# A written order of 3,500 steps, and a table of which half tile is masked where, exchanged for another of the same pieces

## The chip, the cores and the metric

The kernel runs on one core of a Trainium2 chip. The time is device microseconds of that core for one execution. Before the change it is 446.86 us, the median of 3 runs (444.54 to 447.4). The engines are TensorE (PE in the profile, with its weight loads as PEld), VectorE (DVE), ScalarE (ACT), GpSimd (POOL) and SyncE (SP), whose queue issues nearly all DMAs.

## The reference

Attention with a threshold, and then a maxout feed-forward layer, all in float32 at the interface:

```python
# q, k, v: 8 batches x 8 heads x 576 rows x 64
scores = (1 / sqrt(64)) * q @ k.T
thresh = max(scores, axis=-1, keepdims=True) - tau          # tau = 0.02
scores = where(scores >= thresh, scores, -1e9)
attn = exp(scores - max(scores)); attn = attn / (sum(attn) + 1e-9)
x = (attn @ v) with the heads side by side                  # 4608 tokens x 512
h = maximum(maximum(x @ w1, x @ w2), x @ w3)                # 768 wide
out = h @ w_out
```

## The kernel before

**Tiles and stages.** Two by two, 16 groups of four heads (a quad; two quads are one batch) go through attention. A step is 128 query rows of a pair of heads, and has two half tiles of 128 x 576 scores, one for each r; there are 144 steps and 288 half tiles. PE transposes q and k (tile `tp`, evacuated to `qt` and `kt`; `qs` is `qt` with its partition halves exchanged), and makes the scores (`sc`) of a half tile in one of four PSUM banks. DVE copies them, negated, to SBUF (`z`) and takes the row's extreme in the same instruction. ACT makes the exponentials. POOL multiplies by the reciprocal of the sum into `P` (bf16), a DMA transposes `P` into `ptq` (nine DMAs for one quad), and PE multiplies with v (`o`, evacuated to `xt`). From four such products a batch's x is complete, and the feed-forward layer runs in 18 pieces of hidden width (`ph`, three for each 128 of the width, evacuated to `hm`, `hm` and `hT`), then as products with w_out (`po`, to `ob`, stored to `out`). The last batch is done in two parts, so that it has 36 smaller pieces.

**How a half tile is masked** is one digit for each of the 288 in the table `MASKED`:

| digit | DVE | ACT | POOL | reads the bank after DVE's pass |
|---|---|---|---|---|
| 0 | maximum, threshold | two passes (Prelu, Exp) | | nobody |
| 2 | maximum | two passes | | ACT's first pass |
| 1 | maximum, mask-and-sum | one pass | | nobody |
| 3 | maximum, mask-and-sum | one pass | | ACT's pass |
| 5 | maximum, threshold, mask-and-sum | one pass | | ACT's pass and DVE's second |
| 4 | maximum, threshold | one pass | two instructions (`far<-z,th`, `z<-z,far`) | nobody |

In the code these are `masked` (L368), `on_pool` (L371), `direct` (L374), `threshold` (L400), `exponents` (L416), `marked` and `moved` (L434, L440) and `numerators` (L462). The mask-and-sum of DVE is one `scalar_tensor_tensor` that reads `z` twice (digits 1 and 3) or the bank and `z` (digit 5). In the first two quads (`loose`, L364) no reciprocal is taken: the exponentials go straight to `P`, and the sums come from products with `ones`.

**The order.** A string, `ORDER`, is walked from left to right; each letter issues the next piece of its kind. All engines' instructions are tied to their engine's order (`_Ordered`), so the string sets what stands behind what on PE, DVE, ACT, POOL and in SP's queue. The letters that matter here: `S` a half tile's scores with the bank's number, `T` transposes, `O` a product with v, `F` and `B` the two halves of a piece of the feed-forward layer; `m` maximum, `s` threshold, `k` mask-and-sum, `e` and `n` the passes of ACT, `G` ACT's pass of a half tile that POOL has masked; `b` and `C` POOL's two masking instructions, `p` POOL's normalizing, `z` a weight cast on POOL; `t` the transposing DMA, `l` a piece of loading q, k or v, `g` a weight load, `o` a store.

```python
elif what == "m":
    c, r = line["m"].pop(0)
    maximum(c, r)
...
elif what == "t":
    turned(next(ts))
...
elif what in "pqylQ":
    next(flows[what])
```

A letter that waits holds up everything behind it on its engine or queue, and nothing on the others.

Of the kernel before, what the change touches and what calls it, by code (L numbers as in the profile page):

```python
# [48 lines left out]
ORDER = """
lllllllllT1laclT0qqalS3qqclmS2lS1mS3lsmeT0lbmT2nlS1CsalsS3amleqmlqecylGcS0snS3tymyeS2qnsmqeS0bmeS1mCeT3smlaS  # L50
2lknS1qlS0GsmS3ntqmnmbT1emtT0eCcS3anssS0mbT2eS1mqeS3mT0CGctnssmaqGktS1besS0smS3ntyS2memeyCtsnsS3mnS1myS2lGbT
0elmS3qetscT1CnmS0atmeS2qS1ssnsmbGklS0eCgmetmeqmeS1lsnsS0skbS2lemlGqmS1tnysnsS0memS2CeskT1teczO3GmnyskS1Lbsm
eS3tmCES2emT1tO0embakCeS1swnktS0nqS2GmO3ntkbGsmyT1LtCrmS0esS3cpGtS2smpeS1rsmepgmngbemlS2qnslkO3pElmCelrsS2sw
elS0mpnlO3kGpkeT2zrsS1ramLS2mpgeO3stpmnperO1sEqknqswS0LyS3meT1EztO0cesrmpeS1twpnT3mpS0aF2gsemqS3nsBzsmT1eF0r
psgchS3teyBpmS2nS1pnmF3petmBqF2nrsvBepstvS1hpS0nmS2ztnrS1smznF3mteBprsF2evpS0temF3pnBmyS1npvBgemF0lhT2rkBpng
S3valS1emF2qlesBmlpS0evT3F1snrmS2peBscpS0emF3znssmBegkO2htknO0srservpeztF1wxS3nqF2mS0eprBstnpmBnF3zvS0hgS1pe
lmF2eplrBmepgBvF0nysS1veBpmnS2F3khnzBmS1ssrevpgS0S2mtpnT3kepF1mBanmT3qS0tevzT2ssrS1mazteS2mS0ncpS1tesrF3mqek
pteS2smnBprmntprmeS1yS0septmF2upssmuqelT3kS1yelS0smnBlprnslpmlnO1kqleprcO0tupuepS2twnS3ymS1xmepF0sS2nrsmpBnm
yS3hbS1smeF2ptT0meF3ysaBskT1elqrF0rvnBlCcBelS2vhlF1pGmS0tpBersmqT3eS2vtpS0ameF1pssF3mnbBknBpF2rhvT0tBnpcS3ey
svF1tnS0mCBersS2tvnF3pmnS1ptBremF0yhsmpS2GtS3spsmF1epBmnoBqsrveS2lqF3eslvS0petmBpnS1mF2phrmS0eptS3smnS1pBmey  # L60
S0snmF3bemF1tCBnsvBnkF0teF2rsrvpBhBepvS1etbO3mnpvnO1psrkeptS2xwS0GpmT1S3arCtsmS2nmF1eqokGplS3eS0rslmeBplmnpl
srmS2uptS3umS0qnT1moF2ebskleCtT3ersBmecpaS0kupT1uO3mepctO2GkqnrsrleS1wplS0xmS3qlnF2mpteBsmpeS0kT1phS3nsmN2ap
mtnrkpS0jsS3rtrsemF2yeS1mBonyssmpS3eF0vptS1nsmyBepF2rmnptS3vnS1psmeBtqsS0meF3pshsrS1mlpnBmlS2epS0svlepF1lmnT
3bBtmnF2qvnF0BrcepS1hsrT3splBmepF2lassvS1CnlS3metS0pBmnF1vnqS3remqT2BespcF0hslBmpGS2lvbS3elrmS1pntF0mCeF2mT3
eBskptBavS1eF3ssqhmT0nBysS1nvtF2yncyT3BqerrF0vpaBGpmS2tS3hpmF1ntqF0rsmeBpnBvptO3esvpeO2rklpnlerS1pwxtS0nymS3
emS2tyyeS1mqS0nmF3pemplesmF1leklnsBrktpekeS0pS2umuBetmnrT3kpO2uorssknlpO0erlcupriS3wxS1pemF2tpnS0myeBmS1ohyS
3slpemT2S0lepmF1tnpsmF3aBrkpBnsvS0teF2rbsmnS1BpvnS0shCmS3temS2epS1smtnF0pmT3GyBmbF2nrsrvS1eptBssmeCF0ceT1lBa
pvlF3hF1kptGBsBnrvpF2nrS0vpteS3mpS1eBmptnF0smqhS3sreBpmS1nptvF2eS3mqT0nBsmqleF1vqlS3ecBpleS2srmtnpS0mhpO3snm
tO2ekekT1ywxF0arS2rssyS3nbmF1eBmynplBvnS2plsF3svepT0tmBnpS1chCS2tresmF0S3empF1GmBqnT2srsvBpaS3rveptS0meqS1mS
2npS3meF0ptmepsnssmT2tS1qncBbekleCO2lsmunlrrO3skulqerlS0pwxlS1GpmoS3F2emptnspsmS1nprBnmpesrpS3uF1pumS0tnpBme  # L70
F2bF3hsBpeoS0veCS1tmnBN2myetssrekyS1vjpF0tGmS2pnBrkptS3hF1smeS0yminpBrsF3svebT2tBmaCS1vnS2snmbS0emS3pF1GsmS2
pemBCtnF0mF3hsrrssT2pnBcpT1eBvlpaS2evF0pF1GmqT3BnlcBhrlkS2peF3lvS0eprtmBnS1mqnF2tsrqsS0meBqveF1tpmhS3npBssmF
0eptvT2S3parkF1etqBemBS2qvhS3nsmpS1S0empF2nrsstmF3peBmbeS1skBnCsO0mervnO1pGvptrS2wxpS3nmytS1ersmS0ynyF2mplem
plnS1spetS0mT3epBrscnptmepT3S1katO0uqrsumqeO3lkpnoeS1wyS2xmS0npT3mF1elcetrsmS3pnBkeplmelS0ysursF2kptuS3meBpm
S0hF1syrkepT3oS2matBpessS3mF0nqvF2nqrsmBtnBpsvnF1pS3rhBbemF0tevS2pS3epmF1nCBtmeF2srsvBnbS3knS0phmBGF1pmeF3sC
rtsBrveBnvT2pS0hcS1pGF3mptF2emBpnsS0rsvptnS1mpT3eBrmaF0tpeS3vpS1nsmBtqnF2ssmqhT3BrebscS0eS1vpF3nmpF2nBsmCteB
rvS1hS0psnmF2pGmBtT1ervT3pS0acF2pnS1mtqT3smT0aqBecS3qS1veqS0nmF2emerskS3peBmepmnS1ktbF0ussrkuepoS3remBpmeCS1
nsS2umO3pukGpoO1ersmpeS2twpnS0smyxO3tnrsmyO2epskntynS1rwpS0ermN3tbxmnCssS1jF2pGmiS3peBsrmS0pthS1sepmF3nF2pts
mBnpF0sveS1treS3pmeBpsF1metbBnsvF3ChBnBvO2nbrvS1nCwS0GmF3S2rpGmS1psmBeF0pstrshmBpeS2sveS1tbmS3nCF0mnF2snsS1m
pBGsmpBeF3rrstbvF1hBnCF0veBpGBvS2phrS3npmtO1epsmF0xptF2nsBebrF1vBnCBvS3hpS0GmF1ptF2rmepBnsBptvO0epvO3ntwS1xr  # L80
S0pmF3psmtbF2seCkBGBurpupoF1uF0thF3uvF1vF0hoF2vF1vF3hF2vF0vF1hF3vF0vF2hF3vF0vF2hF1vN0vO3jO2iwO1xO3wF2xF1uF3h
oF2vF1vF0hF3vF1vF2hF0vF3vF2hF1vF3vF2hF1vF0vF3hF2vF1vN3uoF2jiF1uofd
"""


# [895 lines left out]
```

## Time and profile before

| | |
|---|---|
| median of 3 runs | 446.86 us |
| profiled execution, time | 447.12 us |
| profiled execution, span | 445.3 us |
| granted TensorE clock | 1.00 in every stage |
| PE, weight loads | 424.0 us (95%), 312.6 us (70%) |
| DVE | 385.6 us (87%) |
| ACT | 400.6 us (90%) |
| POOL | 360.7 us (81%) |
| DMA packets | 88.50 MB, mean 199 GB/s |

Busy time is that of one profiled execution. In a table of stages the share of busy time tells which engine sets a stage's length; in a list of instructions in order of time, the square bracket is the idle time of the engine before the instruction and what ended it. Source lines are of no use here, since every instruction of these engines is recorded at the helper's line L102: the groups are told apart by their tiles.

### The profile page before, as it was taken

The page shows a single profiled execution, that of the slowest core. Times are in us where ns is not written, and L with a number is a line of the kernel's source. Part 1 is how long each engine was busy: PE and PEld are TensorE (multiplying, and loading weights), DVE is VectorE, ACT ScalarE, POOL GpSimd, SP SyncE. Part 2 cuts the span into 40 slices and gives each one's busy share as a digit, 9 for nine tenths or more (in the row PEclk, how much of TensorE's full clock was granted, in tenths as well). Part 3 has the DMA queues.
Part 4 walks back from the last instruction along what each step waited for, and adds up shares of the span by engine and source line. Part 5 has one row for each costly group of instructions (what it writes and reads, how often), then busy time and mean ns, then how long its engine had stood idle before and what let it go on. Part 6 is the DMA issues. An engine that isn't in the chain of part 4 may idle for free.

```text
span 445.3 us, 14407 instructions
## 1 busy us (share of the span) xinstructions
PE 424.0 (95%) x5268; PEld 312.6 (70%) x5270; DVE 385.6 (87%) x1217; ACT 400.6 (90%) x824; POOL 360.7 (81%) x460
## 2 busy tenths in 40 slices
PE   7777899999999999999999998999999999999996
PEld 6454457766678776877688676787688876786873
DVE  4999999989899999998999895899899998887442
ACT  3999999999999999999999897999999999996431
POOL 2898999778999898899797897899989889898100
PEclk9999999999999999999999999999999999999999
DMA  7999999999999999999999999999999867659412
GB/s 176 266 212 244 215 300 237 222 222 290 209 223 161 243 228 249 221 241 222 203 238 235 173 217 251 249 197 182 157 247 184 136 107 177 132 97 139 129 38 83
DMA packets 213959, 88.50 MB, mean 199 GB/s; under 512 B 189184, under 2 KB 202240, under 8 KB 213888
## 3 DMA queue, kind: packets, MB, share of 16 engines
q1 hardware_dynamic: 213360, 86.96, 96.3%
q8 instruction: 41, 0.67, 0.6%
q10 hardware_dynamic: 528, 0.62, 0.5%
q14 instruction: 30, 0.25, 0.2%
HBM read 35.65 MB, written 9.44 MB: 101 GB/s over the span
## 4 chain that ended last, share of the span: by engine, by line
PE 69%; DVE 8%; POOL 6%; DMA 6%; issue 5%; ACT 4%; SPq 1%; POOLq 0%; DVEq 0%; ACTq 0%
PE ph L102 28%; PE sc L102 23%; PE po L102 8%; PE o L102 8%; DVE z L102 5%; POOL P L102 4%; DMA ptq<-P 3%; DMA qm<-in_q_dram 3%; PE tp L102 3%; ACT z L102 2%; POOL qs L102 1%; PE warm L102 1%; SPq L102 1%; ACT P L102 1%; POOL vb L102 1%
## 5 line engine op out<-in xcount | busy, mean ns | idle before, releaser
L102 DVE TENSOR_SCALAR_CACHE_REDUCE z<-sc 128x576 f32<-128x576 f32 x250 | 183.2, 752 | 13.7 <-PE sc L102 11.7
L102 POOL TENSOR_SCALAR P<-z,rs 128x576 bf16<-128x576 f32 x214 | 166.4, 790 | 25.1 <-DVE rs L102 12.4
L102 PE MATMUL sc<-kt,qs 64*128 64x256 f32 (+2 forms) x640 | 176.8, 412 | 5.9 <-DVE z L102 2.9
L102 PE MATMUL sc<-kt,qt 64*128 64x320 f32 (+2 forms) x640 | 178.3, 423 | 3.8 <-DVE kt L102 1.5
L102 PE MATMUL ph<-xt,w 64*128 64x288 bf16 (+2 forms) x2160 | 170.9, 283 | 0.8
L102 PEld LDWEIGHTS <-w 64*128 64x128 bf16 (+1 forms) x2160 | 125.9, 94 | 34.1 <-PE ph L102 4.4
L102 ACT ACTIVATE z<-z,th 128x576 f32<-128x576 f32 x153 | 114.7, 768 | 1.4 <-DVE th L102 1.0
L102 PEld LDWEIGHTS sc<-kt,qs 64*128 64x128 f32 (+1 forms) x640 | 91.0, 175 | 22.8 <-DVE z L102 6.3
L102 PEld LDWEIGHTS sc<-kt,qt 64*128 64x128 f32 (+1 forms) x640 | 90.5, 175 | 17.3 <-DVE z L102 6.1
L102 ACT ACTIVATE z<-z 128x576 f32<-128x576 f32 x139 | 93.6, 675 | 0.2
L102 ACT ACTIVATE z<-z,nm 128x576 f32<-128x576 f32 x73 | 55.2, 769 | 1.3 <-POOL z L102 1.2
L102 POOL COPY qs<-qt 64x640 f32<-64x640 f32 (+3 forms) x66 | 44.9, 680 | 11.4 <-ACT qt L102 8.1
L102 PE MATMUL po<-wo,hT 64*128 64x512 bf16 (+3 forms) x454 | 53.4, 354 | 0.3
L102 DVE TENSOR_TENSOR hm<-ph,hm 128x576 bf16<-128x576 f32 (+2 forms) x54 | 37.1, 687 | 14.6 <-PE ph L102 14.3
L102 POOL TENSOR_TENSOR z<-z,far 128x576 f32<-128x576 f32 x35 | 47.1, 1344 | 1.8
L102 ACT ACTIVATE hm<-ph 128x576 bf16<-128x576 f32 (+2 forms) x54 | 31.8, 590 | 11.8 <-PE ph L102 11.4
L102 PEld LDWEIGHTS <-hT 64*128 64x128 bf16 (+2 forms) x456 | 28.7, 95 | 17.8 <-issue 1.2
L102 DVE TENSOR_TENSOR hT<-ph,hm 128x576 bf16<-128x576 f32 (+2 forms) x54 | 37.1, 687 | 2.7 <-PE ph L102 0.7
L102 DVE SCALAR_TENSOR_TENSOR z<-z 128x576 f32<-128x576 f32 x46 | 38.9, 851 | 0.0
L102 PE MATMUL o<-ptq,vb 128*64 128x512 bf16 (+2 forms) x544 | 36.5, 282 | 2.1 <-DMA ptq<-P 2.1
L102 POOL TENSOR_SCALAR far<-z,th 128x576 int8<-128x576 f32 x35 | 28.6, 816 | 6.8 <-DVE th L102 4.0
L102 POOL TENSOR_SCALAR P<-stage,rs 128x576 bf16<-128x576 f32 x38 | 30.4, 807 | 3.8 <-DVE rs L102 1.6
(63 smaller groups left out, 505.8 us busy)
## 6 DMA issues: line engine op xcount, KB each, us to landing
vm<-in_v_dram SPq DMA_DIRECT2D x32, 256.0 KB, 4.9
qm<-in_q_dram SPq DMA_DIRECT2D x15, 512.0 KB, 5.3
km<-in_k_dram SPq DMA_DIRECT2D x15, 512.0 KB, 5.8
out_dram<-ob SPq DMA_DIRECT2D x14, 512.0 KB, 4.2
stage<-in_moe_w_dram SPq DMA_DIRECT2D x9, 512.0 KB, 5.1
ptq<-P SPq DMA_TRANSPOSE x144, 4.3
vr<-in_v_dram SPq DMA_DIRECT2D x16, 128.0 KB, 4.5
stage<-in_moe_w_out_dram SPq DMA_DIRECT2D x3, 512.0 KB, 4.9
```

The costliest lines, as they stand in the source:

```text
L102: ins = fn(*a, **kw)
```

## The change

The two tables are exchanged; nothing else in the program differs. The pieces of work are the same: 288 half tiles, 64 transposes, 40 products, 162 pieces of hidden width, 144 transposing DMAs, the same loads and stores. The digits of `MASKED` go, in number, from 183 to 178 (0), 53 to 58 (1), 6 to 12 (2), 3 to 5 (3), 38 to 33 (4) and 5 to 2 (5). In the first batch (the first 36 digits) they go from 16, 3, 4, 2, 10, 1 to 10, 5, 10, 3, 8, 0. The string has 3,504 signs in place of 3,522, from its tenth on in another order.

```diff
 MASKED = """
-420024032402140400004110405430000044114100451050050000000000011100000000
-110001000101000001040001004000000001141040010411001030000000000040000104
-001001001110010021004004100000010100400001001040000014100040400100000100
-014000011010010100000401400000004000101141001000400000004404004000402045
+423020132420040121044310022420204214114100451000101000010000000040100020
+012000000010110014000000040000000000441000010141001000010040100000000100
+101000001111100014001000010001004004000010011001005401004000001004000100
+114000001110000001000410400000401000101100010010404000004044010040300003
 """
...
 ORDER = """
-lllllllllT1laclT0qqalS3qqclmS2lS1mS3lsmeT0lbmT2nlS1CsalsS3amleqmlqecylGcS0snS3tymyeS2qnsmqeS0bmeS1mCeT3smlaS
...
+lllllllllT3laclT0qqalS1qqclmS3lS0mS2lS1melsmeT3lbnlsS2mCaS0lmelmeS2qlqcGT0skS1atqecqmeyS3mnS0meyyemS2lnsS3kb
...
 """
```

What this moves on the engines is shown at three places. The first is ACT at the start, from the second evacuation of k on (`tp` is the transposed q or k, `qt` and `kt` what they are evacuated to, `sc` a bank of scores, `nm` the extreme, `th` the threshold, `P` the exponentials of the first quad). Before:

```order
L102 ACTIVATE z_221<-sc_214,nm_212 128x576
L102 ACTIVATE P_260<-z_221 128x576
L102 ACTIVATE qt_183<-tp_236 128x320
L102 ACTIVATE qt_183<-tp_251 128x256
L102 ACTIVATE z_232<-z_232,th_267 128x576
L102 ACTIVATE z_249<-z_249,th_267 128x576
L102 ACTIVATE P_260<-z_211,nm_212 128x576
L102 ACTIVATE P_303<-z_232 128x576
L102 ACTIVATE z_276<-sc_263,nm_277 128x576
```

After:

```order
L102 ACTIVATE z_221<-sc_214,nm_212 128x576
L102 ACTIVATE z_233<-sc_218,nm_234 128x576
L102 ACTIVATE P_256<-z_221 128x576
L102 ACTIVATE qt_183<-tp_243 128x320
L102 ACTIVATE z_240<-z_240,th_259 128x576
L102 ACTIVATE z_264<-sc_230,nm_265 128x576
L102 ACTIVATE P_256<-z_211,nm_212 128x576
L102 ACTIVATE qt_183<-tp_294 128x256
```

Of the passes shown, three of six now read a bank of scores (`sc`) where two of seven did, and the second evacuation of q stands four instructions behind the first.

The second is SP's queue around the load of q for quad 8 (`qm_3175` before, `qm_2789` after). `ptq_2708` before and `ptq_2694` after are the transposed `P` of quad 5, `ptq_3200` that of quad 6; `ob` is a block of output. Before:

```order
L102 DMA_TRANSPOSE ptq_2708<-P_3071 128x9x128
L102 DMA out_0_dram<-ob_2295 64x2x1024
L102 DMA vm_2804<-in_v_dram 64x4x256 x2
L102 DMA q8_3176<-in_q_dram 128x4x64
L102 DMA k8_3178<-in_k_dram 128x4x64
L102 DMA_TRANSPOSE ptq_3200<-P_3143 128x9x128
L102 DMA out_0_dram<-ob_3197 64x2x1024
L102 DMA qm_3175<-in_q_dram 128x2x512
```

After:

```order
L102 DMA_TRANSPOSE ptq_2694<-P_2824 128x9x128
L102 DMA k8_2792<-in_k_dram 128x4x64
L102 DMA qm_2789<-in_q_dram 128x2x512
L102 DMA_TRANSPOSE ptq_2694<-P_2860 128x9x128
L102 DMA_TRANSPOSE ptq_2694<-P_2926 128x9x128
L102 DMA_TRANSPOSE ptq_2694<-P_3048 128x9x128
L102 DMA_TRANSPOSE ptq_2694<-P_3088 128x9x128
L102 DMA out_0_dram<-ob_2253 64x2x1024
```

The load stood behind all nine transposing DMAs of quad 5, one of quad 6 and two stores; now it stands behind five of quad 5 and ahead of the other four and of both stores.

The third is SP's queue at the end of quad 9 (`ptq_4857` before, `ptq_4827` after; `vr` is a part of v). Before:

```order
L102 DMA_TRANSPOSE ptq_4857<-P_5061 128x9x128
L102 DMA vr_5197<-in_v_dram 64x8x64 x2
L102 DMA_TRANSPOSE ptq_4857<-P_5195 128x9x128
L102 DMA_TRANSPOSE ptq_4857<-P_5230 128x9x128
L102 DMA_TRANSPOSE ptq_4857<-P_5294 128x9x128
```

After:

```order
L102 DMA_TRANSPOSE ptq_4827<-P_5109 128x9x128
L102 DMA_TRANSPOSE ptq_4827<-P_5177 128x9x128
L102 DMA_TRANSPOSE ptq_4827<-P_5209 128x9x128
L102 DMA_TRANSPOSE ptq_4827<-P_5270 128x9x128
L102 DMA vr_5343<-in_v_dram 64x8x64 x2
```

The two loads of v that stood ahead of the last three transposing DMAs of the quad stand behind the last.

More of the change, by code (lines that the diff above doesn't have):

```diff
@@ L49 @@
 ORDER = """
-lllllllllT1laclT0qqalS3qqclmS2lS1mS3lsmeT0lbmT2nlS1CsalsS3amleqmlqecylGcS0snS3tymyeS2qnsmqeS0bmeS1mCeT3smlaS
[L51 to L79, printed above, removed]
@@ L80 @@
-pBGsmpBeF3rrstbvF1hBnCF0veBpGBvS2phrS3npmtO1epsmF0xptF2nsBebrF1vBnCBvS3hpS0GmF1ptF2rmepBnsBptvO0epvO3ntwS1xr
-S0pmF3psmtbF2seCkBGBurpupoF1uF0thF3uvF1vF0hoF2vF1vF3hF2vF0vF1hF3vF0vF2hF3vF0vF2hF1vN0vO3jO2iwO1xO3wF2xF1uF3h
-oF2vF1vF0hF3vF1vF2hF0vF3vF2hF1vF3vF2hF1vF0vF3hF2vF1vN3uoF2jiF1uofd
+lllllllllT3laclT0qqalS1qqclmS3lS0mS2lS1melsmeT3lbnlsS2mCaS0lmelmeS2qlqcGT0skS1atqecqmeyS3mnS0meyyemS2lnsS3kb
+lT1emlnS0mCtaS2smT3nS1sqemT0tGsycS2akT3nqS0nmesymS1tqemqecT0tbamS3eCS0smtnmeS3T1kGS2snS0smtbemCemgnS3klnS2bl
@@ new lines @@
+mGS0tecCT3asmS1eykS3qGtsmeqmeteskS2bnS1mS0tnmqeCT2smnS3temqemS0lyGscS1lnS3mzlS2esmtebmnS0mCnlS3smnS2tnS1mbeO
+0sCmGkeS3bemtLkCS1nS2mGO0mEekT1GsrtssO3mpawpetS1kbLS0remO3tCemnsT0kgS1pEscT2gnplmaS0qeT2rlwqO1elscqGlkS3yleS
+2mplLrsS0mntpS1mnpS3reszmO2empeO0pmEgnkqS3tnwS1pLrsS2smpeT0myO3eysmEtpskaS2S1ezwetremT3pF0ecpBnsF2myzF3hsgBn
+tBqvnF0rnS2vptBermpS1hkpS2eS3mngpsrS1mnpT0mazsmS3esF0sseqrgmT1S2ntpcS3nspmF1eBysrmpBetS2vzeS3smeF0pgBnptmF2h
+zvBnF3stnrbS0vF1eCmBnBsegrF2vzlhS0GBpgF1nlmqO3etvpeO0srkqnpBwxpS2evS0ztnF3rmnpBmS1epsS0rlhmzF2elmBpnlsvF0npg
@@ new lines @@
+BleprS3vS1gepmS0tnpS2mepmS1nF3yssmF0emBeS2khT1zsnsBrmS3evtF2armBeqsT1nvT3tzS0escS2pamtS1npsS0mnF3ptmepmeT1S2
+ncS0tersS1rmpeBmqtnsmqnS0F2plureplmS1uylskBnplmelkS0qelsO1upmluprtseO3kyepS2wxS0pnmF3tnbS1rsmeBprmS2eS0CshmF
+1eT3myBatF2vnT0pT3cGBtyF1qsavS0epkF3tnS2pBnmlBhyssrsS0mlpeS1rtsnpvF2empF3eBsbmBtnrvT1qF0hcS2qeF3stqemS1npBmB
+lnpsS2vlepF1rstvS0npBmeCS3monF2slhsBmpGlS0vyF3nlrmBpelS1sveptS2rsF0mnypS3nmS1perBmyS2hspsmF3nS0ptmeBsrsmF2bn
+F1sevtpBnBpvS3etrCF0hmS2eBslmbF1elvT3CnBtsaO0vpnkO2GptrGS1pwxS3pemT2tS0nmqS1emytS3nssF0rrmpeomyeS1ylcpT3nBlm
@@ new lines @@
+palnkqS1lursS3remlF2petsmpuS1snbkT3S0eptBercpemO3CnmuO1sktpGurS0wxqoS2meS3qtmeS1psmnF0pT2emBptS3asrskF1hqS2m
+nBpmeS0S3pvntS2snprmN1eposmelpmS0elsrF3spmjlF2ekBbinS1svpS0etrmpBemS3pnS1ssmCF0hnmBF3evT1tGF2rcpBnkBpnS1rvS0
+hprmS3etT2pssF1semyBemtS0avqS3nF2smlpnS1mlBqestrF0mnqS3svnT1pBeprF2chBspmtnS1yvF3pemS2tpnT0S1meBtrsamF2evT0q
+BtecF1phS3kqT0elS2malBpnF3lvF0eqlsrBmeqtS1svnS2psBmnpF3khF1ynBtsrmBpevO2eprskeptO3vnpnlS1weyS0trmxS2pnmS3yeF
+1rympemptS2nS0pnmT3BelmelcF2elklukS0utkS3eBsrrempempO1uskptusO3erkpnoS0lrxwpS2nlmS1peF3ompS0elmBpnlsS2mhS1bt
@@ new lines @@
+ssmeS0yF3meS2meCBtmF1nF0rGssvpBBkpS2thsvF3eS0ymnBtrmpT2eS1rvpaS0mnytF2qmS3eqBssnsmS0pnvF1peT3mT2BlakS0htqF2s
+rcnF1qmeBpS3evpBemF2teF0rvpS3nskS1peBmBhrtsmS3pnF2svpeS1mF0tebBsrmnpS3veT1CBlmnO2lsnsscblO3nkphrGS0wptF1xmpT
+2eBrrCstaS0vF3nmS2peBsmpeS1F0vGptS2mepBmT3ythS1rcS2nyF0spnmF3nsprBsmeT1ytBvqeS2vpS0almnpS3lS1meqlF2rempnsmT3
+qeBklpetcS0erkS3qntmO1purusmpO0nspkeopS3xlwS2elS0rmpeF1lsmpnlsmnS2tskeF0bBerstmeykBuS2ChS3umF0nyF1osmpnBtrS2
+psGvN3permtpekS0pjBstemF3pnvS2S0nribmT1BaspmS2thS1sysreCmF0eF3mBpessBvetqS2veS1qnmS0pF3GmS2pmeBtF1mhT0rnsS2c
@@ new lines @@
+pS3epmT0BasstsF2nvbF0nmT1CBlersBclnS3pvlF1hrpmS2leBpstmnS0qF3veS2pmnBmnqF1F0vGtBknS3S2sshrmpBeF1rpveT3BpmtaS
+0evpS3emF2tqF1nmS0nrskBpS3smhBepmF2nS0ktbBerrssvpO3empeO1kptnveS0CswxS2nmS3pnmS0ytGmS1T2resrF3rpmecyynS0plmS
+2eplBsmntpmeT1qkuO0tapusO2srkepleorS1wxS3qtemS0pS2nmpF1emtqnskT3peBssrcnpmS0uS3plumF2nplF1meBtrssBphS3pnvS2l
+eyF0rmoT1eBmtpaS3svF2peS1smeqtF0mnBqkBhbS1esvS2nF3myyF0nCmS1terrS2mepBssGsF1bvBnmBphF3kpteT2F0vnBpceBCvtS1hF
+2srnrmS3pGT0BmpaF1srspevS3tS0epmF2nptBmS3npvS0emtqBnT1mqF3hsBcnbS0srsveS2CS1meS3mepF0rGsF2mpBesmptBnvF1pT3hs
@@ new lines @@
+rkBtpaS0veT2S3pmeF1ctqT0BamqS2eS0vqnS3mS1nrmF2pnsmpeT0rsmBnptkeqS3cuF1sepmutkS3esrS2epmS0onpBmnkeS2srmpuO3rs
+umpeO0opsknbeO1trweyO2xktnynS3wpN0ermptxspnS3CeF1trmS2jBspGmiS3yF0hspmS2epBtsnmS1pnF3rvS2tbesmBeCF0mnS1svS2p
+GmO3pnrssmF1petBrwpBshS2petvF3nS0pmBetmbS2nF1vCS0nssmBGF3mbS2rhsrCF0emS1eBspmF2npvBGBstbvS3eF1ChmS0nBsmpF2eF
+3spvGBntbrS0vS1epmO2mCeBxsS1khS2pnF0rrmeF3ptBmGpBssknF2ptF1evBeprBrvhF0ptnS3vpS2nmBptrO1svpeO3mptF0xwepnktF3
+rpBptBuuoF1uF0hF2uvF1voF0hF3vF2vF0hF3vF1vF0hF3vF2vF1hF3vF0vF2hF1vN0vO1jO3iwO0xO2wF3xF2uF0hoF1vF2vF3hF0vF2vF3
@@ L83 @@
+hF0vF1vF3hF0vF1vF2hF0vF3vF2hF1vF3vN1uoF0jiF1uofd
 """
```

## The prediction

> **What bounds the kernel now.** I read the page's busy line first, then the busy time by stage, then the waits of the stages in which PE is idle, and last the instructions in order of time at those waits.
>
> ```profile
> span 445.3 us, 14407 instructions
> PE 424.0 (95%) x5268; PEld 312.6 (70%) x5270; DVE 385.6 (87%) x1217; ACT 400.6 (90%) x824; POOL 360.7 (81%) x460
> ```
>
> Four engines are above 80%, so the average says little. By stage (length, then PE, PEld, DVE, ACT, POOL):
>
> ```profile
> 0.00:12.00 12.00, 9.40 (x98) 7.72 (x98) 5.96 (x26) 4.92 (x9) 4.03 (x11) 1.00 0.79 177
> 12.00:62.00 50.00, 40.47 (x406) 24.55 (x408) 48.47 (x157) 49.49 (x85) 45.76 (x54) 1.00 1.12 241
> 62.00:100.00 38.00, 37.67 (x500) 26.94 (x500) 33.88 (x107) 37.50 (x79) 31.86 (x43) 1.00 1.14 240
> 100.00:270.00 170.00, 165.52 (x2132) 122.31 (x2128) 158.76 (x505) 164.08 (x344) 151.49 (x195) 1.00 1.11 223
> 270.00:410.00 140.00, 139.75 (x1842) 109.21 (x1840) 124.86 (x396) 132.81 (x285) 124.37 (x158) 1.00 0.90 173
> 410.00:445.30 35.30, 31.17 (x306) 21.88 (x304) 13.72 (x31) 11.76 (x26) 3.18 (x4) 1.00 0.30 88
> ```
>
> From 12 to 62 us there is no feed-forward work to give PE: it idles 9.53 us, while ACT is idle 0.51 and DVE 1.53 of 50. That stretch is as long as the passes of ACT and DVE that the order puts ahead of the first feed-forward piece. From 62 us on PE is the bound. It idles 0.33 us to 100, 4.48 to 270, 0.25 to 410, and 4.13 at the end, where the change moves little. So there are two things to win: the length of the early part, and the 4.48 us. The waits of 12 to 62 us say the same of the banks, PE waiting for DVE and hardly for ACT:
>
> ```profile
> PEld sc L102 <- DVE z L102: 10.2, 15, 2.0
> PEld tp L102 <- ACT z L102: 0.7, 1, 0.7
> PE tp L102 <- ACT z L102: 0.2, 1, 0.2
> PE sc L102 <- ACT z L102: 0.2, 1, 0.2
> ```
>
> Of the 4.48 us four stalls make 4.02; each row has PE's idle time before it in brackets:
>
> ```profile
> 126.25 0.46 PE L102 MATMUL tp<-identf,qm 64*128 64x64 f32 x8 [0.73 <-DMA qm<-in_q_dram]
> ...
> 174.33 0.46 PE L102 MATMUL tp<-identf,qm 64*128 64x64 f32 x8 [0.72 <-DMA qm<-in_q_dram]
> ...
> 248.20 0.53 PE L102 MATMUL sc<-kt,qs 64*128 64x320 f32 x1 [0.51 <-POOL qs L102]
> ...
> 269.44 0.93 PE L102 MATMUL o<-ptq,vb 128*64 128x512 bf16 x11 [2.06 <-DMA ptq<-P]
> ```
>
> **The change: sums of work.** The prices are these rows (busy total, mean ns):
>
> ```profile
> L102 DVE TENSOR_SCALAR_CACHE_REDUCE z<-sc 128x576 f32<-128x576 f32 x250 | 183.2, 752 | 13.7 <-PE sc L102 11.7
> L102 ACT ACTIVATE z<-z,th 128x576 f32<-128x576 f32 x153 | 114.7, 768 | 1.4 <-DVE th L102 1.0 <-DVE rs L102 0.2
> L102 POOL TENSOR_TENSOR z<-z,far 128x576 f32<-128x576 f32 x35 | 47.1, 1344 | 1.8
> L102 DVE SCALAR_TENSOR_TENSOR z<-z 128x576 f32<-128x576 f32 x46 | 38.9, 851 | 0.0
> L102 DVE TENSOR_SCALAR th<-nm 128x1 f32<-128x1 f32 x226 | 30.4, 145 | 0.8
> L102 POOL TENSOR_SCALAR far<-z,th 128x576 int8<-128x576 f32 x35 | 28.6, 816 | 6.8 <-DVE th L102 4.0
> L102 ACT ACTIVATE z<-sc,nm 128x576 f32<-128x576 f32 x14 | 10.1, 734 | 3.7 <-DVE z L102 3.7
> ```
>
> By the digits, POOL masks 5 half tiles fewer: 5 x (0.816 + 1.344) = 10.8 us less. DVE's mask-and-sum goes from 61 to 65 (digits 1, 3, 5), 4 x 0.851 = 3.4 us more, and its thresholds from 226 to 213 (digits 0, 4, 5), 13 x 0.145 = 1.9 us less: 1.5 us more. ACT makes two passes for 190 half tiles in place of 189, one of 0.768 us more. PE's work does not change. So nothing is taken off the engine that bounds after 62 us, and the two that bound before it get a little more; what can be won is in the order.
>
> One row speaks against taking masks from POOL to DVE. A mask-and-sum on DVE and, beside it, POOL's first masking step:
>
> ```profile
> 43.34 0.75 DVE L102 SCALAR_TENSOR_TENSOR P<-z 128x576 bf16<-128x576 f32 x1
> ...
> 43.59 1.11 POOL L102 TENSOR_SCALAR far<-z,th 128x576 int8<-128x576 f32 x1 [0.51 <-DVE th L102]
> ```
>
> POOL's 0.816 became 1.11 us, 0.29 more. The digits 1 and 3, whose mask-and-sum reads SBUF twice, go from 56 to 63; at 0.29 each, 7 give POOL 2.0 us back, and its gain is 8.8 rather than 10.8. I take 8.8: it is idle time there either way, since POOL bounds neither stage. [...]
>
> **The early part.** Counted in the string up to its first `F`, before has 56 half tiles' scores and 79 large passes of ACT (`e`, `n`, `G`: 41 + 26 + 12), after 58 and 81 (45 + 26 + 10). ACT, the fullest, gets 2 x 0.768 = 1.5 us more before PE is fed, which was here:
>
> ```profile
> 69.89 0.72 PE L102 MATMUL ph<-xt,w 64*128 64x288 bf16 x8
> ```
>
> In exchange PE has two half tiles behind it, which take 0.97 us by the chain of waits:
>
> ```profile
> 347.07 0.98 PE ph L102 x16
> ...
> 350.81 0.97 PE sc L102 x8
> ...
> 368.41 2.47 PE o L102 x40
> ```
>
> Net +0.6 us. DVE's count (2 maxima, 2 masks, 9 thresholds fewer) is 1.5 + 1.7 - 1.3 = 1.9, less 0.97: +0.9, of which its idle 1.53 can take some. Ends: +0.9 at the top, and below nothing ACT's idle 0.51 in that stretch, -0.5. I take +0.6. Not in it is that direct half tiles (digits 2, 3, 5), whose bank is freed only after ACT or DVE has read it again, go from 7 to 13 in the first batch; in before PE waited 1.1 us for ACT at such places (the three ACT rows of the waits), 0.16 for each of 7, so six more are 0.9 us of PE's wait in a stretch in which PE is idle 9.5 us anyway. I take nothing; the third rival is where that fails.
>
> **The four stalls.** At 174 us the load of q for quad 8 came late, held in SP's queue behind transposing DMAs and a store:
>
> ```profile
> 165.44 2.33 SPq L102 DMA_TRANSPOSE ptq<-P  x1
> 167.87 0.62 SPq L102 DMA_DIRECT2D out_dram<-ob  x1
> 168.54 0.58 SPq L102 DMA_DIRECT2D qm<-in_q_dram  x1
> ```
>
> Between that load and the transposes that need it, the string has 5 `S`, 2 `O`, 3 `F`/`B` and 2 `T` before, 14, 4, 6 and 4 after. At 0.485 for an `S`, 1.23 for an `O` and 0.49 for an `F` or `B` (the rows above) that is 6.4 us against 14.7 without the `T`s: 8.3 us more for a load that was 0.72 late. This stall goes: -0.72.
>
> At 269 us the last transposed tile of quad 9 is late, and ahead of it in the queue stood two loads of v:
>
> ```profile
> 261.07 1.30 SPq L102 DMA_DIRECT2D vr<-in_v_dram  x2
> 262.46 6.25 SPq L102 DMA_TRANSPOSE ptq<-P  x4
> ```
>
> They now stand behind it: 1.30 us sooner. Between the last `t` and the product there are also one `S` and one `B` more, 0.97 us of work. 1.30 + 0.97 exceeds 2.06, so this stall goes too, if the transfers themselves are no slower: -2.06. The wait for `qs` at 248 us hangs on POOL. By then (six batches) POOL has 23 masks behind it where it had 26, 6.5 us less work, but its queue empties in between; bounds 0 and -0.51, and I take -0.3. At 126 us the load of quad 6 stands as far ahead (6 `S`, 2 `O`, 2 `F`, 1 `B` in both): 0.
>
> What is late next: quad 4's load. Between it and its transposes are 7 `S` and 2 `O`, where 6 `S`, 4 `O` and one `T` more were, 2.0 us less at least.
>
> ```profile
> 60.27 0.36 SPq L102 DMA_DIRECT2D qm<-in_q_dram  x1
> ...
> 68.80 0.46 PE L102 MATMUL tp<-identf,qm 64*128 64x64 f32 x7
> ...
> 119.16 6.95 DMA qm<-in_q_dram
> 168.54 5.66 DMA qm<-in_q_dram
> ```
>
> It had 8.5 us, and loads took 5.66 and 6.95; with 6.5 us the new stall is 0 to 0.5. Two other distances that shrink (quad 5's load, quad 2's product) have no row that prices them; I allow the same again and take +0.6 for all, with 0 and 1.5 as ends.
>
> **Sum.** +0.6 - 0.72 - 2.06 - 0.3 + 0.6 = -1.9 us. The profiled execution's span of 445.3 becomes 443.4, its time of 447.12 becomes 445.2; it lay 0.3 above the median of 446.86, which becomes 445.0. A measurement of this kernel can tell about 1% (4.5 us) from no change, so this is within 1%. The ends of the terms give 443.1 (-0.5, -3.3 with all of the three stalls, 0) to 447.5 (+0.9, -1.75 with 0.72 and half of 2.06, +1.5).
>
> **The rivals.**
>
> *PE's busy time hides room, and the next bound is ACT.* The order then closes also the small waits inside PE's busy stretches. From 62 to 270 us ACT is idle 0.50 + 5.92 = 6.4 us; less one pass of 0.768 this gives -5.7, and 441.2. For it: PE's matmuls overlap, so a busy PE can be waiting. Against: 16 matmuls of `ph` take 0.98 us wherever the chain shows them at their pace, and from 270 to 410 us PE is idle 0.25. [...]
>
> *Stalls only change places.* ACT at 97% and DVE at 93% of 100 to 270 us have little slack to follow a faster PE; the stalls gone are paid back at the loads and products with less distance. 446.9.
>
> *The early part gets longer, because banks are held.* Six more direct half tiles in the first batch each keep a bank for ACT's 0.734, and as ACT is full PE gets the bank later, DVE the scores, and ACT its next pass. If each costs its 0.734 in full, 4.4 us, with the +0.6 above, 451.9: over 1% slower. For it: PE waited 10.2 us for DVE to free banks in that stretch. Against: ACT rows of 1.1 us in all. It decides where each costs over 0.65 us.
>
> **How the numbers follow.** The forecast has 0.40, the room behind PE 0.24, stalls in other places 0.18, held banks 0.18. Faster by over 1% (under 442.4) is the first rival and a little beyond the forecast's lower end, 0.26; slower by over 1% (over 451.3) the held banks, 0.18, and 0.01 for loads that come later still; within 1% 0.55. The range, 440.0 to 451.5, takes in the forecast's own (443.1 to 447.5), the first rival's price and the third's, and leaves out what lies beyond these.
>
> **What would show it.** Right: no idle time before the `tp` that stood at 174 us, under 0.5 us before quad 9's product, PE's first `ph` near 71.4 us (69.89 + 1.5), ACT still over 98% busy in the early stage. Wrong: PE waiting for ACT's `z` in the early part by more than 3 us in all (held banks); a first `ph` before 68 us, or a PE whose busy total falls by several us (room); waits for `qm` or `ptq` at other quads (places changed).

## The result, and the profile after

The changed kernel takes 453.5 us (median of 19 executions, 446.8 to 458.4); the kernel before, on the same chip, 446.1 (19 executions, 442.4 to 449.1). The ratio is 1.0099 with a 95% interval of 1.0075 to 1.0122. The ratio leaves out executions far above a kernel's fastest, here ten of the changed kernel's 19; the two medians over all stand 1.0166 apart. So the change makes the kernel slower by 1.0 to 1.7%, where the forecast was 0.4% faster, and 453.5 lies outside the range.

The first profile of the changed kernel is of its shortest execution (446.79 us), which is as long as a usual one of before. Its busy line, and then the stages (length, then PE, PEld, DVE, ACT, POOL, the granted clock, the DMA share, GB/s):

```profile
span 444.9 us, 14395 instructions
PE 425.5 (96%) x5270; PEld 314.6 (71%) x5270; DVE 389.2 (87%) x1210; ACT 400.2 (90%) x823; POOL 351.8 (79%) x450
```

```profile
12.00:62.00 50.00, 42.20 (x422) 26.42 (x422) 48.17 (x145) 49.44 (x85) 42.00 (x51) 0.97 1.11 239
62.00:100.00 38.00, 35.97 (x462) 24.04 (x460) 31.75 (x104) 35.80 (x77) 34.41 (x43) 1.00 1.17 236
100.00:270.00 170.00, 167.44 (x2174) 128.36 (x2174) 159.67 (x503) 164.96 (x348) 147.38 (x193) 1.00 1.11 228
270.00:410.00 140.00, 139.22 (x1832) 106.31 (x1826) 130.59 (x409) 134.60 (x286) 123.11 (x155) 1.00 0.91 169
```

In the early stage PE is busy 1.7 us more (42.20 for 40.47), and its clock is 0.97, not 1.00. From 62 to 100 us PE now idles 2.0 us where it idled 0.33, from 100 to 270 us 2.56 where it idled 4.48. The two stalls that the prediction priced are gone; there is no bracket at either place (PE in order of time):

```profile
176.17 0.44 PE L102 MATMUL tp<-identf,qm 64*128 64x64 f32 x7
...
268.37 2.17 PE L102 MATMUL o<-ptq,vb 128*64 128x512 bf16 x32
```

A second profile of the unaltered changed kernel (452.8 us, a usual one) has a longer stall than either, at a place where before has none. POOL waits for a transposed tile, DVE for POOL to free a `z` buffer, PE and ACT for what follows from it:

```profile
199.93 0.74 POOL L102 TENSOR_SCALAR P<-z,rs 128x576 bf16<-128x576 f32 x1 [4.70 <-DMA ptq<-P]
200.71 0.76 DVE L102 TENSOR_SCALAR_CACHE_REDUCE z<-sc 128x576 f32<-128x576 f32 x1 [3.44 <-POOL P L102]
...
201.53 0.46 PE L102 MATMUL tp<-identf,km 64*128 64x64 f32 x8 [3.27 <-DVE th L102]
202.53 0.65 ACT L102 ACTIVATE hm<-ph 128x576 bf16<-128x576 f32 x1 [3.20 <-PE ph L102]
```

Right behind it the clock is at half for 3.41 us (the stretch before it and the stretch itself; the clock is the third number from the end):

```profile
199.33:202.74 3.41, 1.21 (x24) 1.01 (x24) 2.03 (x6) 0.21 (x1) 2.61 (x4) 1.00 1.18 237
202.74:206.15 3.41, 3.35 (x26) 2.27 (x24) 2.31 (x6) 3.20 (x7) 3.20 (x6) 0.50 1.03 211
```

SP's queue in the same profile shows what was late. Loads of q, k and v for quad 9 and three stores went out from 187.4 to 191.6 us, and the last three transposing DMAs of quad 6 behind them:

```profile
187.37 0.63 SPq L102 DMA_DIRECT2D out_dram<-ob  x1
188.10 0.54 SPq L102 DMA_DIRECT2D qm<-in_q_dram  x1
188.73 0.90 SPq L102 DMA_DIRECT2D km<-in_k_dram  x1
189.68 0.67 SPq L102 DMA_DIRECT2D vm<-in_v_dram  x1
190.44 1.21 SPq L102 DMA_DIRECT2D out_dram<-ob  x2
191.74 9.23 SPq L102 DMA_TRANSPOSE ptq<-P  x4
```

From issue to landing the six transposing DMAs of 186 to 204 us took 3.3 to 8.0 us, 4.7 in the middle:

```profile
DMA to landing us min/median/max: 3.3/4.7/8.0
```

Two profiles of one program, then, are 6 us apart, and some 5 us of that lie at this one place. The waits over the whole span say that such a place is no accident: DVE waits for POOL's buffers 5.7 and 9.6 us in the two profiles of the changed kernel, and 1.4 us in the second profile of before (in the first, no such wait is listed). Changed kernel, second profile:

```profile
DVE z L102 <- POOL P L102: 9.6, 5, 3.4
POOL P L102 <- DMA ptq<-P: 7.3, 4, 4.7
```

Kernel before, second profile:

```profile
POOL P L102 <- DMA ptq<-P: 2.4, 3, 1.5
...
DVE z L102 <- POOL P L102: 1.4, 3, 0.8
```

### The profile page after: what moved, and what is told of

The parts are those of the page before. It is cut to its first block, busy times and chain, and to the rows that moved or that the text cites. A ratio compares the mean times of both kernels' runs of the same rounds, so it can differ in the third digit from the quotient of the medians.

```text
span 444.9 us, 14395 instructions
## 1 busy us (share of the span) xinstructions
PE 425.5 (96%) x5270; PEld 314.6 (71%) x5270; DVE 389.2 (87%) x1210; ACT 400.2 (90%) x823; POOL 351.8 (79%) x450
## 4 chain that ended last, share of the span: by engine, by line
PE 63%; POOL 12%; ACT 8%; DVE 7%; issue 5%; DMA 3%; SPq 1%; POOLq 0%; ACTq 0%; DVEq 0%
PE ph L102 24%; PE sc L102 21%; PE po L102 8%; POOL P L102 7%; PE o L102 6%; DVE z L102 4%; ACT z L102 4%; DMA ptq<-P 3%; ACT P L102 3%; PE tp L102 2%; POOL w L102 2%; POOL qs L102 1%; PE warm L102 1%; DVE stage L102 1%; SPq L102 1%
## 5 line engine op out<-in xcount | busy, mean ns | idle before, releaser
L102 PE MATMUL sc<-kt,qs 64*128 64x256 f32 (+2 forms) x640 | 179.2, 414 | 4.7 <-ACT z L102 1.9
L102 ACT ACTIVATE z<-z,th 128x576 f32<-128x576 f32 x149 | 112.0, 768 | 1.0 <-DVE th L102 0.6
L102 ACT ACTIVATE z<-z 128x576 f32<-128x576 f32 x141 | 94.9, 675 | 0.1
L102 POOL COPY qs<-qt 64x640 f32<-64x640 f32 (+3 forms) x66 | 46.2, 700 | 12.5 <-ACT qt L102 9.1
L102 DVE SCALAR_TENSOR_TENSOR z<-z 128x576 f32<-128x576 f32 x48 | 42.9, 896 | 0.6 <-ACT z L102 0.5
L102 POOL TENSOR_TENSOR z<-z,far 128x576 f32<-128x576 f32 x31 | 40.2, 1296 | 1.6
L102 PE MATMUL o<-ptq,vb 128*64 128x64 bf16 (+2 forms) x544 | 36.6, 282 | 1.2 <-DVE z L102 0.8
L102 PEld LDWEIGHTS <-vb 128*64 128x64 bf16 x544 | 21.6, 111 | 16.1 <-issue 6.8
```

The costliest lines, as they stand in the source:

```text
L102: ins = fn(*a, **kw)
```

## The experiments

Ratios are to the kernel before on the same chip, with a 95% interval. "Loads" are those of q, k and v.

**Both kernels again, and the two halves of the order.** The string was cut at the first `F`, and the digits with it; each half was combined with the other kernel's. The two half tiles by which the halves differ are made at the seam, so that early_before has 58 ahead of its first `F`, like the changed kernel.

```diff
 # early_before: the order of before up to the first F, then the changed one (the seam)
-elS0mpnlO3kGpkeT2zrsS1ramLS2mpgeO3stpmnperO1sEqknqswS0LyS3meT1EztO0cesrmpeS1twpnT3mpS0aF2gsemqS3nsBzsmT1eF0r
+elS0mpnlO3kGpkeT2zrsS1ramLS2mpgeO3stpmnperO1sEqknqswS0LyS3meT1EztO0cesrmpeS1twpS2nT0msmpsaS2S1etemT3pF0ecpBn
 # early_after: the reverse
```

> The changed kernel unaltered, for a second profile: 19 executions lay between 446.79 and 458.41 us, and the profile at hand is of the shortest. Theory E (the early part): a typical execution is longer ahead of the first feed-forward piece, where the first profile has PE waiting 7.1 us for ACT (4.1 + 3.0) from 12 to 62 us and one stretch of 3.4 us at half the TensorE clock; a typical one has two to four such stretches, and its first ph piece is 3 to 8 us later than 70 us. Theory M (the middle): the first ph piece is near 70 us as before, and 5 us or more are lost from 62 to 130 us, where DVE waits for POOL to free a z buffer (5.7 us in the first profile, nothing before the change). Both: about 451 to 454 us.

> The kernel before, unaltered, for the granted clock of its executions, of which only one is known (1.00). Theory E: its clock stays at 1.00 in nearly all of them, since PE's idle times in the early part are shorter or lie otherwise, and its times stay within 442 to 449. Theory M says nothing of the clock; if the clock falls below 0.99 here as often as after the change, the clock is no part of the cause. Both: about 446 us.

> The order and digits of the changed kernel up to its first feed-forward piece (56 half tiles and the steps ahead of it), and from there on the order of before for all that is left. Theory E: as slow as the changed kernel or slower, 451 to 456 us, clock under 1.00. Theory M: as before or faster, 444 to 448.

> The order and digits of before up to its first feed-forward piece, and from there on the order of the changed kernel. Theory E: the changed order's gains at quads 8 and 9 remain and nothing is lost early, 443 to 446 us, clock 1.00. Theory M: slow like the changed kernel, 450 to 454, with DVE waiting for POOL's release of z from 62 to 130 us.

Measured: the changed kernel again 1.0137 (1.0094 to 1.0180), before again 1.0000 (0.9975 to 1.0025), early_after 1.0087 (1.0052 to 1.0122), early_before 1.0107 (1.0063 to 1.0150). Each half alone costs nearly as much as both, so the loss does not sit in one of them, and the two do not add.

**Exchanging the places of the loads.** Every load got the place (counted in transposing DMAs ahead of it) that it has in the other kernel; nothing else moved. SP's queue at quad 3's loads, for the first of the three:

```diff
-L102 DMA_TRANSPOSE ptq<-P 128x9x128 x5
-L102 DMA vr<-in_v_dram 64x8x64 x2
+L102 DMA_TRANSPOSE ptq<-P 128x9x128 x2
+L102 DMA vr<-in_v_dram 64x8x64
+L102 DMA_TRANSPOSE ptq<-P 128x9x128
+L102 DMA vr<-in_v_dram 64x8x64
 L102 DMA qm<-in_q_dram 128x2x512
-L102 DMA_TRANSPOSE ptq<-P 128x9x128
 L102 DMA km<-in_k_dram 128x2x512
-L102 DMA_TRANSPOSE ptq<-P 128x9x128 x5
+L102 DMA_TRANSPOSE ptq<-P 128x9x128 x8
...
```

> The changed kernel, with its loads of q, k and v alone put back to where they stand in the kernel before (the same number of transposing DMAs ahead of each). Theory 'loads ahead of transposes' (bulk loads now queued ahead of transposing DMAs make these land late, POOL then keeps its P buffers, DVE waits for z, PE idles, and the clock goes to half for 3.4 us): 4 to 7 us back, 446 to 449, and no half-clock stretch near 200 us. Rival 'held banks' (the direct half tiles of the first batch): the early part is untouched, so 452 to 453.5. Rival 'the order of the work itself': no change either, about 453; the two stalls at 174 and 269 us may come back and make it 454 to 456.

> The reverse: the kernel before, with the loads of q, k and v at the places that they have in the changed kernel. Theory 'loads ahead of transposes': 450 to 452, with a half-clock stretch behind a late transposed tile. Both rivals: 445 to 446, or 443 if the two stalls that the prediction priced go with the loads.

> The order of the kernel before up to the first feed-forward piece and of the changed one from there (450.1 when it ran), now with the loads of q, k and v of the later part at the places of the kernel before as well. Theory 'loads ahead of transposes': 445 to 447, the later part's 4 to 5 us go. Rival 'held banks' says nothing of the later part; rival 'the order of the work itself': 449.5 to 451, unchanged.

Measured: 1.0283 (1.0248 to 1.0319), 1.0238 (1.0212 to 1.0263) and 1.0192 (1.0166 to 1.0218). All three are slower than what they were made from. That before's places are the better ones whatever the order is refuted; that a load's place matters is shown, by up to 2.4%. In the first of them PE lost 5.8 us at one point, where the loads of the diff now stand ahead of transposing DMAs #2 and #3 of quad 1: these landed at 48.75 and 51.37 us, in the changed kernel at 41.80 and 43.16 (engines in order of time):

```profile
48.83 0.78 ACT L102 ACTIVATE P<-z,nm 128x576 bf16<-128x576 f32 x1 [3.14 <-DMA ptq<-P]
51.47 0.76 DVE L102 SCALAR_TENSOR_TENSOR P<-z 128x576 bf16<-128x576 f32 x1 [5.31 <-ACT ob L102]
...
52.95 0.79 PE L102 MATMUL sc<-kt,qt 64*128 64x256 f32 x1 [5.77 <-DVE z L102]
```

**Held banks.** In one kernel the thirteen direct half tiles of the changed kernel's first batch read SBUF; in the other, five of before's became direct.

```diff
 # after_no_direct: the first 36 digits of the changed kernel
-423020132420040121044310022420204214
+401000110400040101044110000400004014
 # before_more_direct: the first 36 digits of the kernel before
-420024032402140400004110405430000044
+420024232402142420204110405430000244
```

> The changed kernel, with the thirteen direct half tiles of the first batch made to read their scores from SBUF (ten of digit 2 become 0, three of digit 3 become 1): their banks come free with DVE's pass; DVE gets ten thresholds more, 1.45 us. Rival 'held banks': at least the 4.4 us of the prediction's third rival back, 444 to 449, PE's and its weight loads' waits for ACT's z before 62 us under 1 us, and no half-clock stretch near 35 us. Theory 'loads ahead of transposes': 452 to 454.5 (DVE's 1.45 us more at the most).

> The kernel before with five more direct half tiles in the first batch (five of digit 0 become 2; twelve direct in place of seven; DVE has five thresholds fewer, 0.73 us). Held banks: longer PE waits for ACT's z before 62 us, a half-clock stretch more in many executions, 1.1 us (what the changed kernel's thirteen gave back, 2.9 us, times 5 of 13) to 3.7 us (5 x 0.734) over before. If direct half tiles cost nothing in themselves: 445 to 446.

Measured: 1.0072 (1.0039 to 1.0105) and 1.0070 (1.0042 to 1.0099). Both look like held banks: perhaps some gain where they go (the intervals of 1.0072 and 1.0099 overlap), a loss where they come. In before_more_direct the first `ph` came at 74.0 us (69.9 and 71.2 in two profiles of before), so an order that was not written for them does pay. The changed kernel also has PE's waits for ACT in the early stage, 3.0 us of PE and 4.1 of its weight loads (none and 0.5 in after_no_direct):

```profile
PEld sc L102 <- DVE z L102: 4.2, 8, 0.9
PEld sc L102 <- ACT z L102: 4.1, 3, 2.2
PE sc L102 <- ACT z L102: 3.0, 3, 1.7
```

But the first `ph` of after_no_direct came at 72.9 us (72.4 in after_no_direct_quad9, below), 2 us or more behind the changed kernel's 70.4 and 70.3. So if it gained, it gained later than the banks; the runs without loads, below, bear on that.

**Single moves of loads.** Quad 9's three loads were put back behind transposing DMA #9 of quad 6 (in the changed kernel, and in after_no_direct), and in before only the two moves that the prediction had priced were made.

```diff
 # after_quad9_loads, SP
+L102 DMA out_dram<-ob_3561 64x512 x2
+L102 DMA_TRANSPOSE ptq<-P 128x9x128 x3
 L102 DMA qm<-in_q_dram 128x2x512
 L102 DMA km<-in_k_dram 128x2x512
-L102 DMA vm<-in_v_dram 64x4x256
-L102 DMA out_dram<-ob_3566 64x512 x2
-L102 DMA_TRANSPOSE ptq<-P 128x9x128 x4
-L102 DMA vm<-in_v_dram 64x4x256
+L102 DMA_TRANSPOSE ptq<-P 128x9x128
+L102 DMA vm<-in_v_dram 64x4x256 x2
 # before_two_loads, SP at 168 us and at 261 us
+L102 DMA qm<-in_q_dram 128x2x512
 L102 DMA_TRANSPOSE ptq<-P 128x9x128
 L102 DMA out_dram<-ob 64x2x1024
-L102 DMA qm<-in_q_dram 128x2x512
...
+L102 DMA_TRANSPOSE ptq<-P 128x9x128 x5
+L102 DMA vr<-in_v_dram 64x8x64 x2
 L102 DMA_TRANSPOSE ptq<-P 128x9x128 x2
-L102 DMA vr<-in_v_dram 64x8x64 x2
-L102 DMA_TRANSPOSE ptq<-P 128x9x128 x5
```

> The changed kernel with three loads alone put back: q, k and a part of v of quad 9, which it has ahead of the transposing DMAs #7 to #9 of quad 6, stand behind #9 again, as in the kernel before. Theory 'late transposed tile at 200 us' (in the second profile of the changed kernel #7 took 8.0 us, POOL waited 4.70 us for a P buffer, DVE 3.44, PE 3.27, and the clock went to half right behind): 2 to 4 us back against 453, 449 to 451, and no half-clock stretch near 200 us. Rival 'loads belong to their order' (every exchange of loads so far made the time longer): 453 to 457, with PE waiting for q or k of quad 9 near 201 us.

> Both edits: no direct half tiles in the first batch (450.2 alone) and quad 9's three loads behind #9 of quad 6. If the changed kernel's loss is held banks early and the late transposed tile at 200 us, and the two add: 446.5 to 448. If the loads belong to their order: 450 to 454.

> The kernel before with the two moves of loads alone that the prediction priced: q of quad 8 ahead of the first transposing DMA of quad 6 and of a store (0.72 us), and the two loads of v that stood ahead of the last three transposing DMAs of quad 9 behind them (2.06 us). The prediction's terms: 2.8 us less, 443.2 against 446. Rival 'stalls only change places': 445.5 to 446.5.

Measured: 1.0103 (1.0056 to 1.0149), 1.0072 (1.0049 to 1.0094), and 1.0000 (0.9976 to 1.0024). The place at 200 us, mended alone, gives back nothing that can be measured; its stall was one of several that an execution may or may not have. The profile of the mended kernel has no stall there and has two others: 2.79 us between the starts of two matmuls of one product at 91 us and 2.02 at 269 us, both for a transposed tile. The second is quad 9's product, the very place where the prediction took a stall to be gone (PE idle for 1.61 us; 2.06 in before).

The last run is the prediction's main term by itself, and it is worth nothing that can be measured. Both stalls are gone from its profile, and another is there, at a load that neither move touches:

```profile
129.60 0.46 PE L102 MATMUL tp<-identf,km 64*128 64x64 f32 x8 [1.31 <-DMA km<-in_k_dram]
...
175.28 0.44 PE L102 MATMUL tp<-identf,qm 64*128 64x64 f32 x7
...
268.85 2.17 PE L102 MATMUL o<-ptq,vb 128*64 128x512 bf16 x32
```

The second profile of the unaltered kernel before (444.63 us) shows one reason: it has neither stall.

```profile
174.13 0.44 PE L102 MATMUL tp<-identf,qm 64*128 64x64 f32 x7
...
266.89 2.17 PE L102 MATMUL o<-ptq,vb 128*64 128x512 bf16 x32
```

**Without the loads.** From batch 2 on, quads 4 to 15 use the data of quads 2 and 3, and their loads are not issued; all other work is done.

```diff
         L = Ls[g] = dict(g=g, b=b, qd=qd, first=first)
+        if b > 1:
+            L.update({n: Ls[2 + qd][n] for n in ("q", "k", "q8", "k8", "vm")})
+            if qd == 0:
+                L["vr"] = Ls[2]["vr"]
+            for _ in range(4 if qd else 8):
+                yield
+            return
```

> The kernel before, without the loads of q, k and v from batch 2 on (quads 4 to 15 use the data of quads 2 and 3; everything else is done, so the time is that of the same work with fewer transfers). It is the other half of the next run. Theory 'loads and transposing DMAs get in each other's way': 441 to 444, since the stalls at 126, 174 and 269 us go. If loads cost nothing: 445 to 446.

> The changed kernel without the same loads. Theory 'half of the loss is held banks in the first batch, the other half loads and transposing DMAs that meet differently in each execution': 3 us (0.65%) over the kernel before without loads, not 7, and executions that lie closer together. If the loss is in the order of the work and not in the transfers: 5 to 7 us over it.

> The changed kernel with neither: no direct half tiles in the first batch, no loads of q, k and v from batch 2 on. Theory of two halves: within 1 us of the kernel before without loads. If something else in the order costs: 3 us over it, as after_no_direct is over the kernel before.

> The changed order up to the first feed-forward piece and the one of before from there, without the loads of q, k and v from batch 2 on (the two parents without them: 0.9954 and 1.0011 of the kernel before). If the early part is worth what the prediction took, +0.6 us: 0.997. If the 0.57% lies in the early part (banks, clock): 1.001. With its loads this kernel was 1.0087, so anything near 1.0 says that the meeting with the loads was 0.8% of it.

> The reverse without the same loads: the order of before up to the first feed-forward piece and the changed one from there. If the early part is only +0.6 us, the later part holds the rest of the 0.57%: 1.000. If the early part holds it all: 0.9955. With its loads this kernel was 1.0107.

| | with the loads | without |
|---|---|---|
| before | 1.0000 | 0.9954 (0.9936 to 0.9972) |
| changed | 1.0099 and 1.0137 | 1.0011 (0.9988 to 1.0033) |
| after_no_direct | 1.0072 | 1.0037 (1.0022 to 1.0051) |
| early_after | 1.0087 | 1.0003 (0.9973 to 1.0033) |
| early_before | 1.0107 | 1.0044 (1.0021 to 1.0067), of eleven; a twelfth execution took 854.32 us |

Leaving the loads out gives the kernel before 0.46%, after_no_direct 0.35%, and the other orders 0.63 to 1.26%. The changed kernel's distance to before falls from 1.0 to 1.4% to 0.57% (1.0011 - 0.9954, give or take 0.3). So about half of the loss (0.4 to 0.8 of 1.0 to 1.4%) goes when the later loads go. By the medians of all executions it is more: 1.7% with the loads (453.5 to 446.1 us, and 453.09 to 445.45) and 0.5% without (444.44 to 442.07). That this part is what the loads and the transposing DMAs do to each other is the likely reading, since a transposed tile lands later where there are loads; in order, before, changed, and the two without loads (median of 144, us from issue to landing):

```profile
ptq<-P SPq DMA_TRANSPOSE x144, 4.3
```

```profile
ptq<-P SPq DMA_TRANSPOSE x144, 4.5
```

```profile
ptq<-P SPq DMA_TRANSPOSE x144, 3.5
```

```profile
ptq<-P SPq DMA_TRANSPOSE x144, 3.6
```

Both kernels gain alike in this median (0.8 and 0.9 us), so it does not show why the changed one loses more by its loads. The changed kernel without loads, from 100 to 270 us, has a DMA share of 0.72 where it had 1.11:

```profile
100.00:270.00 170.00, 168.80 (x2192) 129.91 (x2194) 161.26 (x507) 166.53 (x351) 149.05 (x195) 1.00 0.72 139
```

PE idles 1.20 us there in place of 2.56, and ten of the twelve executions lie between 443.1 and 444.9 us.

The third row speaks against the held banks. Without the later loads, taking the thirteen direct half tiles away makes the kernel 0.26% slower (give or take 0.27), not faster; it also adds ten thresholds, 1.45 us of DVE, and the first `ph` is at 72.6 us for 71.2. The first batch is the same in both columns, so in this order the direct half tiles cost nothing on balance; a price of the held bank that is smaller than what the thresholds save is not excluded. What after_no_direct may have gained with the loads, it would have gained by meeting them at other times; no run shows that apart.

What is left without loads, 0.57% or 2.4 us, is not settled. Its halves again add up to more than the whole: the changed early part alone costs 0.49% (1.0003 against 0.9954, give or take 0.35), the changed later part alone 0.90% (1.0044, give or take 0.29). Each half was written for the other one, and what the seam costs is not measured.

**PE kept busy in the early wait.** Half tile 28 ends 2.1 us before DVE reads it, and PE then waits for a bank; its scores are made four times over.

```diff
-        for x in (1, 0):
+        for x in (1, 0) * (4 if (L["g"], idx, r) == (1, 5, 0) else 1):
```

> The changed kernel, with the scores of half tile 28 (the last before PE's wait of 2.08 us at 34 us) made four times over in place: 1.4 us of work that PE does while it would wait, and DVE reads that half tile 2.1 us after its end. Nothing else is moved. Theory 'the clock goes to half behind a stretch of 3.4 us with about 2 us of idle time': no half-clock stretch near 36 us, the mean clock of the executions 0.003 to 0.004 higher (0.9930 for 0.9896), 1 to 1.7 us less time. Rival 'the clock has no part in it': time and clock unchanged.

Measured: 1.0131 (1.0098 to 1.0165). The half-clock stretch at 36 us is gone, and the mean clock of the executions is 0.9955 for the changed kernel's 0.9898, more than forecast; before has 0.999. The time lies between the two ratios of the unaltered changed kernel (1.0099 and 1.0137). So a higher clock early brought no gain that can be measured; the forecast gain of 0.2 to 0.4% is neither seen nor quite ruled out. In its profile the filled kernel is 0.6 and 0.9 us ahead of the two profiles of the changed one at 43 us (start of DVE's 37th maximum), and by 61 us it has lost that, and more. It had a late transposed tile of quad 1, queued behind a load of k, and the clock at half behind that (59.8 to 66.6 us):

```profile
60.67 1.65 PE L102 MATMUL o<-ptq,ones 128*64 128x512 bf16 x11 [2.84 <-DMA ptq<-P]
```

No version beats both kernels: the best with all its work is before_two_loads, at before's own time.

## Why the prediction was wrong, step by step

**The bound** was read rightly: PE is at 96%, and first ACT, then PE set the stages.

**Sums of work.** POOL was to lose 8.8 us and lost 8.9 (360.7 to 351.8), in part by luck: its masking lost 9.5 us, and its copies of `qs`, which the sum held fixed, took 1.3 more. The slower masking beside DVE's mask-and-sums that read SBUF twice is in both profiles. POOL's first step has a mean of 747 ns wherever none of them runs at the same time (28 steps of before, 21 of the changed kernel), and of 988 and 1143 ns where one does (10 and 12). The means over all agree: this step went from 816 to 901 ns, DVE's mask-and-sum from 851 to 896, the second of which the sum had not counted (DVE went up 3.6 us, not 1.5).

```profile
L102 DVE SCALAR_TENSOR_TENSOR z<-z 128x576 f32<-128x576 f32 x48 | 42.9, 896 | 0.6 <-ACT z L102 0.5
...
L102 POOL TENSOR_SCALAR far<-z,th 128x576 int8<-128x576 f32 x31 | 27.9, 901 | 10.1 <-DVE th L102 7.6 <-ACT z L102 0.4
```

**The early part, +0.6.** The first `ph` came at 70.4 and 70.3 us in two profiles (71.4 was named as the sign), where before has 69.9 and 71.2; without the later loads it came at 71.2, and at 70.5 in before. So one profile more or less moves it by more than the term, and it confirms neither the size nor the direction. The executions do say something: without the later loads the changed early part alone costs 0.49%, some 2.2 us (0.6 to 3.7 by the intervals), ahead of an order that was not written for it. The direction was right there, and +0.6 was probably too small. The sign named for held banks came true (3.0 us of PE's and 4.1 of its weight loads' waits for ACT, the mark being 3 in all), the delay of the first `ph` did not. So the third rival's price, 451.9, was the nearest of all to the result, by luck: its reason is one that the runs do not bear out in this order.

**The stalls, -0.72 and -2.06: here the sum failed.** In the profile at hand the stalls went, as worked out, but taking them away is worth 0.0% (before_two_loads, give or take 0.24), not 0.63%. The step that failed is taking a wait's length in one profile as a term of the sum, that is, as time that the median would win. The runs show three things in its place. The stalls are not in every execution: of four profiles with before's order and loads at both places, the first has both, early_after has the first alone, at 2.69 us, and before_again and before_more_direct have neither (0.2 us at the most). A wait for a load need not lengthen the execution: the first profile of before is 1.3 us ahead of the second at 77 us (start of DVE's 61st maximum), waits at 126 and 174 us for q, and is level with it at 178 us (the 131st); the stall at 269 us did set it back, by 2.4 us. And other waits come where these are gone, such as the 1.31 us for k in before_two_loads. How much each of the three takes from the 2.78 us is open.

**What was left out of the sum.** Of each load that the order moves ahead, the prediction asked how much sooner its own transposes on PE can begin, and not what is then queued behind it. q of quad 8 went ahead of four transposing DMAs of quad 5, and was booked as -0.72; quad 9's three loads went ahead of three of quad 6, and were not in the sum at all. Its term for such things, +0.6 with 1.5 as the end, only held loads that come late. The part of the loss that goes with the later loads measured 0.4 to 0.8%, 2 to 3.5 us. Which loads make it is open: quad 9's, put back alone, gave nothing back that can be measured.

**The wait for `qs`, -0.3,** did go (no such wait of PE at 248 us), and is too small to be told from nothing.

**The rivals.** "Stalls only change places" comes nearest to the mechanism of the loads' half of the loss, at a price of zero for it. The longest stall that came (3.27 us of PE, at 200 us in the second profile) was longer than those that went: there a late transposed tile reached PE through POOL's `P` buffers and DVE's `z` buffers, and stopped all of them. Room behind PE's busy time: PE's busy total rose by 1.5 us. In the early stage, with its stretch at half the clock, it rose by 1.7; outside it stayed as it was (383.3 for 383.5 us), which is no sign of room.

## What to carry to other kernels

A stall in one profile is one draw of a spread (of four profiles two have the first stall, one the second): before it is priced, ask a second profile of the same program whether it is there. Where transfers fill the DMA engines (a share of 1.11 here from 100 to 270 us), a load that is moved ahead can be paid for by what is queued behind it (5.8 us of PE at one point of after_loads_of_before), so count the transposing DMAs that it passes, and follow a late one through the buffers that it keeps. How much of a loss hangs on the transfers, and how much on the order of the work, shows when the transfers are left out of both kernels.
